# A vector sum issued four slots later, and a block pair's opening products issued ahead of a plain block

## The chip, the cores and the metric

The kernel runs on one core of a Trainium2 chip. The metric is the device time of one execution in microseconds. A core has a matrix engine (TensorE, PE in the profile; its weight loads are PEld), a vector engine (VectorE, DVE), a scalar engine (ScalarE, ACT), a general engine (GpSimd, POOL) and a queue engine for transfers (SyncE, SP). Each engine works through its own instructions in order, and semaphores tie the engines together.

## The reference

Two stages follow each other. The first is a linear attention over 8 batches, 8 heads, 576 positions and 64 features:

```python
q_p, k_p = phi(q), phi(k)          # relu, times cos and sin of the position
kv  = einsum('bhsf,bhsd->bhfd', k_p, v)
x   = einsum('bhsf,bhfd->bhsd', q_p, kv) / (q_p . sum_s(k_p) + 1e-6)
```

With the heads side by side, x is (8, 576, 512). The second stage mixes positions with a product of rank 32 and then applies two dense layers:

```python
u   = x + transpose(transpose(x) @ U @ V)
out = u + relu(u @ w_ch1) @ w_ch2          # 512 -> 2048 -> 512
```

## The kernel before

Matrix work is done in bf16 with float32 sums in PSUM, which has eight banks. The 576 positions of a batch are worked on as 512 (four chunks of 128) and a tail of 64; the tails of two batches go together.

**The order of the work** is written out by hand. The list `slots` holds steps for TensorE, and `put(n, ...)` hangs other steps behind slot n: VectorE sums, casts, attention units, transfers. At the end, a loop runs each slot, then what hangs behind it (in the order of the calls of `put`), then what `behind` has gathered. Within a slot, each engine receives its instructions in that order.

**The first dense layer** of batches 0 to 5 is made of plain blocks: `g1_main` (L569) makes one of 16 blocks of 128 hidden features with four matmuls of 512 columns (L579) and a relu on ScalarE (L588). The target banks turn over; at the place of the change they are g0 and g1.

For batch 6, `units` holds eight plain blocks (0, 8, 1, 9, 2, 10, 3 and 11) and, for the others, four *block pairs* p = 4 to 7 (block p with block p + 8). A block pair is one step of a scheme that multiplies 2 x 2 blocks with seven products instead of eight. `g1_cross` (L651) issues product i as two matmuls of 256 columns (L676). Products 1 and 2 go to the two halves X and Y of one bank, g0 or g1 by turns; products 6, 7 and 4 add to X later; 5 and 3 go to another bank. `g1_join` (L682) takes the results out: for "P1", ScalarE copies X to a buffer `kept` (L129); for "C11", VectorE adds that copy and Y (L611) into the hidden layer. `opened` issues products 1 and 2 and the joins P1 and C11; `sixth` issues product 6, again into X, and its copy. `third`, `fifth` and `closed` issue the rest.

The scheme needs sums of parts of its inputs, made on VectorE: `uT_sum` (L634, also L611 through `diff`) makes four of them from the transposed u, `w1_sum` those of the weights. `uT_s[b, 4]` is read by product 4 alone, which `closed` issues.

**The second dense layer** of the batch before, 5, runs between these steps: `half_part` (L862) issues eight matmuls of 256 columns (L891), and the same scheme gives it seven products for each half batch. `beside_g` puts one half part ahead of each unit. Its results are copied by ScalarE (L129) or added by VectorE (L847), and `hid_sum` (L833) makes sums of the hidden layer on VectorE.

**The attention of batch 7** runs in the same slots. `x_unit` (L415) issues eight matmuls of 65 columns (L422) into a tile of two banks that carries the name X too (another than the half X of a block pair) and exists once; VectorE takes the reciprocal (L412, L413) and multiplies (L432, into `x_tl` for the tail, into `x_bf` for the others), and after that the tile may be written again. Five of them follow each other, in every second slot; `A_unit` (L445) comes behind them.

With `at` the first slot of batch 6's first layer, a slot list of the stretch reads: `at + 4` a half part, `uT_sum(b6, 4)`, the tail's `x_unit`; `at + 6`, `at + 8`, `at + 10`, `at + 12` a half part and an `x_unit` each; `at + 13` the plain block 11 and the opening of block pair 4; `at + 14` a half part; `at + 15` product 6 of that pair and `A_unit`; `at + 19` the step `closed` of that pair.

Of the kernel before, what the change touches and what calls it, by code (L numbers as in the profile page):

```python
# [17 lines left out]
def kernel(  # L18
# [550 lines left out]
    def g1_main(b, j, half=False):  # L569
        if b not in hid:  # L570
            hid[b] = pool.tile([P, NJ, 512], BF16, tag="hid", bufs=2, name="hid")
        g_ps = g_open.pop((b, j), None)
        d0 = 0 if g_ps is None else 2
        if g_ps is None:
            g_ps = ps.tile([P, 512], FP32, tag="g", bufs=3, name="g_ps")
        if half:
            g_open[b, j] = g_ps
        for d in range(d0, 2 if half else 4):
            nc.tensor.matmul(  # L579
                out=g_ps.rearrange("p (c t) -> p c t", c=4),  # L580
                lhsT=w1_bf[:, d, j * P : j * P + P],
                rhs=uT[b][:, d, :, :],
                start=(d == 0),
                stop=(d == 3),
            )
        if half:
            return
        nc.scalar.activation(  # L588
            out=hid[b][:, j, :], in_=g_ps, func=AF.Relu, bias=0.0, scale=1.0
        )  # L590
# [19 lines left out]
    def diff(o, x, y, op=ALU.subtract):  # L610
        V_.tensor_tensor(out=o, in0=x, in1=y, op=op)  # L611
# [19 lines left out]
    def uT_quarter(b, d, n):  # L631
        return uT[b][:, 2 * d : 2 * d + 2, 2 * n : 2 * n + 2, :]

    def uT_sum(b, i):  # L634

        if not uT_s:
            t = pool.tile([P, 2, 4, 2, 2, P], BF16, tag="vst", bufs=1, name="uT_s")
            for n in range(4):
                for m in range(2):
                    uT_s[B - 2 + m, n + 1] = t[:, m, n]  # L640
        x, y = {
            1: lambda: (uT_quarter(b, 0, 1), uT_quarter(b, 0, 0)),
            2: lambda: (uT_quarter(b, 1, 1), uT_s[b, 1]),
            3: lambda: (uT_quarter(b, 1, 1), uT_quarter(b, 0, 1)),
            4: lambda: (uT_quarter(b, 1, 0), uT_s[b, 2]),
        }[i]()
        diff(uT_s[b, i], x, y)
# [3 lines left out]
    def g1_cross(b, p, i):  # L651

        if (b, p) not in cross:
            if b not in hid:
                hid[b] = pool.tile([P, NJ, 512], BF16, tag="hid", bufs=2, name="hid")
            of_x, of_z = CROSS[p % 2] if b == B - 1 else (("g0", "g1")[p % 2], "T")
            xy = psum.tile([P, 512], FP32, tag=of_x, bufs=1, name="c_ps")
            cross[b, p] = {"X": xy[:, 0:256], "Y": xy[:, 256:512], "of_z": of_z}  # L660
        w = cross[b, p]
        if i == 5:
            z = psum.tile([P, 512], FP32, tag=w["of_z"], bufs=1, name="c_ps")
            w["Z"] = z[:, 0:256]
        cs = slice(p * P, p * P + P)
        to, lhs, rhs, first = {
            1: lambda: ("X", W1[0], uT_quarter(b, 0, 0), True),
            2: lambda: ("Y", W1[1], uT_quarter(b, 1, 0), False),
            3: lambda: ("Z", w1_s[4], uT_quarter(b, 1, 1), False),
            4: lambda: ("X", W1[3], uT_s[b, 4], False),  # L670
            5: lambda: ("Z", w1_s[1], uT_s[b, 1], True),
            6: lambda: ("X", w1_s[2], uT_s[b, 2], False),
            7: lambda: ("X", w1_s[3], uT_s[b, 3], False),
        }[i]()
        for d in range(2):
            nc.tensor.matmul(  # L676
                out=w[to].rearrange("p (c t) -> p c t", c=2), lhsT=lhs[:, d, cs],
                rhs=rhs[:, d], start=(first and d == 0), stop=(d == 1),
                skip_group_check=not first,
            )  # L680

    def g1_join(b, p, i):  # L682

        w, lo, hi = cross[b, p], slice(0, 256), slice(256, 512)
        top, low = hid[b][:, p, :], hid[b][:, p + 8, :]

        def relu(o, x):
            nc.scalar.activation(out=o, in_=x, func=AF.Relu, bias=0.0, scale=1.0)

        if i == "C11":  # L690
            diff(top[:, lo], w["P1"], w["Y"], ALU.add)
        elif i == "C22":
            diff(low[:, hi], w["P5"], w["X"], ALU.add)
            relu(low[:, hi], low[:, hi])
        elif i == "C12":
            diff(top[:, hi], w["U2"], w["Z"], ALU.add)
            relu(low[:, lo], w["X"])
            V_.tensor_scalar(out=top, in0=top, scalar1=0.0, scalar2=None, op0=ALU.max)
        else:
            if (b, "kept") not in cross:  # L700
                cross[b, "kept"] = pool.tile(
                    [P, 2, 3, 256], FP32, tag="q_pT" if b == B - 1 else "q_p", bufs=1,
                    name="kept",
                )
            n = ("P1", "U2", "P5").index(i)
            w[i] = cross[b, "kept"][:, p % 2, n]
            cast(A_, w[i], w["Z" if i == "P5" else "X"])
# [630 lines left out]
    def put(at, thunk):  # L1338
        todo.setdefault(at, []).append(thunk)
# [11 lines left out]
    def g1(b, j):  # L1351
        return lambda: g1_main(b, j)
# [22 lines left out]
    for b in range(3, B - 2):  # L1375
        at = len(slots)
# [15 lines left out]
    b6, b7 = B - 2, B - 1  # L1392

    def opened(b, p):
        g1_cross(b, p, 1)
        g1_cross(b, p, 2)
        g1_join(b, p, "P1")
        g1_join(b, p, "C11")
# [24 lines left out]
    def crossed(*steps):  # L1423
        def go():
            for f, b, p in steps:
                f(b, p)

        return go
# [10 lines left out]
    at = len(slots)  # L1439
# [4 lines left out]
    ):  # L1444
        put(at + sl, lambda i=i, half=half: w1_sum(i, half))
    for i in range(4):
        put(at + 1 + i, lambda i=i: uT_sum(b6, i + 1))
    units = [g1(b6, j) for p in range(3) for j in (p, p + 8)] + [g1(b6, 3)]
    units.append(lambda: [g1_main(b6, 11), opened(b6, 4)])
    units.append(crossed((sixth, b6, 4)))  # L1450
    for p in range(5, 8):
        units.append(crossed((opened, b6, p), (fifth, b6, p - 1), (third, b6, p - 1)))
# [17 lines left out]
    at = len(slots)  # L1470
# [26 lines left out]
    at = len(slots)  # L1497
# [16 lines left out]
    at = len(slots)  # L1514
# [59 lines left out]
```

## Time and profile before

| | |
|---|---|
| median of three runs | 295.01 us (294.25 to 295.41) |
| the profiled execution's own time | 294.76 us |
| its span, first to last instruction | 293.0 us |
| granted TensorE clock | 1.000 |
| DMA | 56.18 MB, mean 192 GB/s |
| matmuls of L579 with 512 columns, into g_ps | 378, mean 379 ns |
| matmuls of L891 with 256 columns | some 273 ns each |

A row of the timeline gives the start and the duration in us, the engine, the line, the operation, output and inputs, and in brackets the idle time of the engine before it with what ended that. Ends of matmuls are modelled: a matmul's recorded duration reaches beyond the start of the next one, so the time that TensorE needs for a piece of work is read from one start to the next. The list of waits gives, for each pair of lines, the idle time in total, the number of times and the longest. The view of stretches gives, for a stretch, its length, the busy time of each engine with its count of instructions, the granted clock and the load of the DMA engines.

### The profile page before, as it was taken

The numbers are of one execution on the slowest core, as the hardware profiler recorded it, in microseconds if no ns is written. First come the engines' busy times: TensorE is split into PE (matmuls) and PEld (weight loads), VectorE is DVE, ScalarE is ACT, GpSimd is POOL, SyncE is SP. The second block draws the span as 40 slices with busy tenths as digits, with TensorE's granted clock in tenths as the row PEclk, the third lists the DMA queues.
The fourth block names the chain that finished last, engine by engine and source line by source line (L and its number), as shares of the span: only waits on it lengthen the run. The fifth ranks groups of instructions, "written<-read, shape, count | busy, mean of one in ns | idle before, by whom it ended". The sixth has DMA issues, their size and how long they took to land.

```text
span 293.0 us, 7309 instructions
## 1 busy us (share of the span) xinstructions
PE 284.9 (97%) x2910; PEld 194.5 (66%) x2944; DVE 206.6 (71%) x503; ACT 169.2 (58%) x353; POOL 56.6 (19%) x92
## 2 busy tenths in 40 slices
PE   8999999999999999999999999999999999999994
PEld 3775564447645446676767666766766888889883
DVE  5976766496876697657547793779957886765773
ACT  2955652176882767578736865497644555567210
POOL 5520400000020002301400501041101313303330
PEclk9999999999999999999999999999999999999999
DMA  6999999999988999999899939984902754336023
GB/s 210 304 254 251 260 163 223 223 332 251 316 178 135 312 231 246 232 313 268 128 231 273 272 72 292 214 284 87 219 2 38 120 116 98 64 93 142 4 103 116
DMA packets 95174, 56.18 MB, mean 192 GB/s; under 512 B 58692, under 2 KB 91844, under 8 KB 95140
## 3 DMA queue, kind: packets, MB, share of 16 engines
q1 hardware_dynamic: 84420, 43.94, 60.4%
q0 software_dynamic: 10528, 11.57, 19.5%
q8 instruction: 23, 0.38, 0.5%
q10 hardware_dynamic: 192, 0.20, 0.2%
q14 instruction: 11, 0.09, 0.1%
HBM read 36.86 MB, written 9.44 MB: 158 GB/s over the span
## 4 chain that ended last, share of the span: by engine, by line
PE 91%; ACT 3%; DMA 2%; DVE 2%; issue 1%; ACTq 0%; DVEq 0%
PE g_ps L579 29%; PE h_ps L891 26%; PE o_ps L759 10%; PE c_ps L676 7%; PE gt_ps L719 5%; PE kv_ps L347 3%; PE x_ps L422 3%; DMA qst<-in_q_dram 2%; PE a_ps L445 1%; PE h_ps L759 1%; PE g_ps L596 1%; PE va_ps L475 1%; PE t_ps L365 1%; ACT q_p L306 1%; ACT k_p L306 1%
## 5 line engine op out<-in xcount | busy, mean ns | idle before, releaser
L579 PE MATMUL g_ps<-uT,w_bf 128*128 128x512 bf16 x378 | 95.4, 379 | 1.2
L588 ACT ACTIVATE hid<-g_ps 128x512 bf16<-128x512 f32 x104 | 61.2, 598 | 58.8 <-PE g_ps L579 57.9
L579 PEld LDWEIGHTS <-w_bf 128*128 128x128 bf16 x402 | 37.5, 98 | 34.5 <-issue 0.2
L891 PEld LDWEIGHTS <-hid 128*128 128x128 bf16 x480 | 45.6, 98 | 9.5
L891 PE MATMUL h_ps<-w_bf,hid 128*128 128x256 bf16 x288 | 37.1, 273 | 0.0
L759 PE MATMUL o_ps<-w_bf,hid 128*128 128x512 bf16 x122 | 29.5, 379 | 0.4 <-issue 0.2
L891 PE MATMUL h_ps<-w_s,S 128*128 128x256 bf16 x208 | 26.5, 272 | 0.0
L131 POOL CAST v_ext<-vst 128x512 bf16<-128x512 f32 (+1 forms) x23 | 15.2, 689 | 58.1 <-DMA vst<-in_v_dram 30.3
L891 PE MATMUL h_ps<-w_s,hid 128*128 128x256 bf16 x192 | 24.9, 273 | 0.0
L847 DVE TENSOR_TENSOR o_sb<-o_sb,h_ps 128x256 f32<-128x256 f32 (+1 forms) x36 | 15.5, 432 | 12.2 <-PE h_ps L891 9.6
L891 PEld LDWEIGHTS <-S 128*128 128x128 bf16 x208 | 20.1, 98 | 4.4
L483 DVE TENSOR_TENSOR u_bf<-x_bf,va_ps 128x512 bf16<-128x512 bf16 x27 | 17.6, 680 | 6.5 <-PE va_ps L475 2.8
L950 POOL DMA_DIRECT2D out_dram<-o_sb x16 | 9.9, 617 | 63.3 <-DVE o_sb L847 50.4
L611 DVE TENSOR_TENSOR hid<-kept,c_ps 128x256 bf16<-128x256 f32 x36 | 14.2, 418 | 10.5 <-ACT kept L129 7.6
L847 DVE TENSOR_TENSOR o_sb<-u_bf,h_ps 128x256 f32<-128x256 bf16 x28 | 11.7, 417 | 13.6 <-PE h_ps L891 13.5
L759 PEld LDWEIGHTS <-hid 128*128 128x128 bf16 x128 | 11.5, 98 | 12.2
L949 POOL DMA_DIRECT2D o_sb<-u_bf x8 | 10.4, 1302 | 34.3 <-DVE rec L413 15.9
L719 PE MATMUL gt_ps<-uT_tl,w_bf 128*128 128x128 bf16 x256 | 16.2, 219 | 0.0
L432 DVE TENSOR_TENSOR x_bf<-x_ps,rec 128x512 bf16<-128x512 f32 x22 | 15.2, 691 | 0.8
L129 ACT ACTIVATE kept<-c_ps 128x256 f32<-128x256 f32 x36 | 12.5, 380 | 5.4 <-PE c_ps L676 5.0
L719 PEld LDWEIGHTS <-w_bf 128*128 128x128 bf16 x256 | 15.1, 98 | 0.7
L306 ACT ACTIVATE k_p<-kst,cosw 128x512 bf16<-128x512 f32 x20 | 14.2, 713 | 0.2 <-DMA kst<-in_k_dram 0.2
(189 smaller groups left out, 455.4 us busy)
## 6 DMA issues: line engine op xcount, KB each, us to landing
qst<-in_q_dram SPq DMA_DIRECT2D x14, 512.0 KB, 6.2
kst<-in_k_dram SPq DMA_DIRECT2D x14, 512.0 KB, 6.7
vst<-in_v_dram SPq DMA_DIRECT2D x12, 512.0 KB, 6.9
out_dram<-o_sb POOLq DMA_DIRECT2D x19, 256.0 KB, 3.9
out_dram<-o_sb SPq DMA_DIRECT2D x16, 256.0 KB, 2.6
w_bf<-in_moe_w_ch_dram POOLq DMA_DIRECT2D x7, 512.0 KB, 13.0
o_sb<-u_bf POOLq DMA_DIRECT2D x8, 256.0 KB, 3.7
qst<-in_q_dram SPq DMA_DIRECT2D x2, 640.0 KB, 14.2
```

The costliest lines, as they stand in the source:

```text
L131: eng.tensor_copy(out=o, in_=i)
L306: nc.scalar.activation(out=o, in_=i, func=AF.Relu, bias=0.0, scale=w)
L432: nc.vector.tensor_tensor(out=x_of(b, c, rows).rearrange("p (g i d) -> p g i d", g=2, d=D), in0=view[:, :, :, 0:D], in1=rec[rows].unsqueez ...
L483: nc.vector.tensor_tensor(out=u_bf[b][:, j, :, :], in0=x_bf[b][:, :, ns], in1=va[b][j].rearrange("p (c n) -> p c n", c=4), op=ALU.add,)
L579: nc.tensor.matmul(out=g_ps.rearrange("p (c t) -> p c t", c=4), lhsT=w1_bf[:, d, j * P : j * P + P], rhs=uT[b][:, d, :, :], start=(d == 0) ...
L588: nc.scalar.activation(out=hid[b][:, j, :], in_=g_ps, func=AF.Relu, bias=0.0, scale=1.0)
L611: V_.tensor_tensor(out=o, in0=x, in1=y, op=op)
L676: nc.tensor.matmul(out=w[to].rearrange("p (c t) -> p c t", c=2), lhsT=lhs[:, d, cs], rhs=rhs[:, d], start=(first and d == 0), stop=(d == 1 ...
L719: nc.tensor.matmul(out=g_ps[:, jj, :], lhsT=w1_bf[:, d, j * P : j * P + P], rhs=uT_tl[pr][:, d, :], start=(d == 0), stop=(d == 3),)
L759: nc.tensor.matmul(out=o[:, cols], lhsT=lhs[:, j, c * P : c * P + P], rhs=w2_bf[:, j, cols], start=(j == 0), stop=(j == NJ - 1),)
L847: eng.tensor_tensor(out=o, in0=x, in1=y, op=ALU.add)
L891: nc.tensor.matmul(out=acc, lhsT=lhs[:, j, :], rhs=rhs[:, j, :], start=(j == 0 and at is not None), stop=(j == 7), skip_group_check=at is ...
```

## The change

Two lines of the schedule differ. The sum `uT_sum(b6, 4)` hangs behind slot `at + 8` instead of `at + 4`. In slot `at + 13` the two steps change places: the four matmuls of `opened(b6, 4)` and its joins are issued first, then the four matmuls of plain block 11 and its relu.

```diff
     for i in range(4):
-        put(at + 1 + i, lambda i=i: uT_sum(b6, i + 1))
+        put(at + (1, 2, 3, 7)[i], lambda i=i: uT_sum(b6, i + 1))
     units = [g1(b6, j) for p in range(3) for j in (p, p + 8)] + [g1(b6, 3)]
-    units.append(lambda: [g1_main(b6, 11), opened(b6, 4)])
+    units.append(lambda: [opened(b6, 4), g1_main(b6, 11)])
     units.append(crossed((sixth, b6, 4)))
```

On TensorE, four matmuls of 256 columns with their weight loads now stand ahead of four of 512 columns. On ScalarE, the copy P1 stands ahead of the relu of block 11. On VectorE, the sum stands behind the first two attention products' reciprocals and multiplications and one sum of the hidden layer, ahead of the third's reciprocals. The instructions of GpSimd and SyncE keep their order.

## Prediction

> **What bounds the kernel now.** I read the page first, from the top: the busy time of the engines, then the chain of work that ended last.
>
> ```profile
> span 293.0 us, 7309 instructions
> ...
> PE 284.9 (97%) x2910; PEld 194.5 (66%) x2944; DVE 206.6 (71%) x503; ACT 169.2 (58%) x353; POOL 56.6 (19%) x92
> ...
> PE 91%; ACT 3%; DMA 2%; DVE 2%; issue 1%; ACTq 0%; DVEq 0%
> ```
>
> TensorE is busy for 97% of the span and makes up 91% of the chain. The change adds and removes no instruction, so all it can do is close holes in TensorE's stream or open new ones. So the next view is the list of waits, for TensorE alone, from 207 us to the end, the stretch that holds batch 6's first layer and everything behind it:
>
> ```profile
> PE c_ps L676 <- DVE hid L611: 0.4, 1, 0.4
> PE x_ps L422 <- DVE x_tl L432: 0.2, 1, 0.2
> ```
>
> Two waits, once each, and each stands beside one half of the diff. The third view is the timeline of all engines around them. The first hole (start in us, duration, engine, line; idle time before it in brackets):
>
> ```profile
> 214.55 0.42 PE L422 MATMUL x_ps<-kv,q_tlT 128*128 128x65 bf16 x8
> ...
> 214.81 0.42 DVE L847 TENSOR_TENSOR o_sb<-o_sb,h_ps 128x256 f32<-128x256 f32 x1 [2.27 <-ACT kv L129]
> ...
> 215.14 0.42 DVE L611 TENSOR_TENSOR uT_s<-uT,uT_s 128x512 bf16<-128x512 bf16 x1
> ...
> 215.59 0.17 DVE L412 TENSOR_SCALAR rec<-x_ps 64x8 f32<-64x8 f32 x1
> 215.67 1.04 PE L891 MATMUL h_ps<-w_s,S 128*128 128x256 bf16 x8
> ...
> 216.03 0.69 DVE L432 TENSOR_TENSOR x_tl<-x_ps,rec 64x512 bf16<-64x512 f32 x1
> ...
> 216.87 0.42 PE L422 MATMUL x_ps<-kv,q_pT 128*128 128x65 bf16 x8 [0.17 <-DVE x_tl L432]
> ...
> 217.92 0.69 DVE L432 TENSOR_TENSOR x_bf<-x_ps,rec 128x512 bf16<-128x512 f32 x1
> 217.99 1.04 PE L891 MATMUL h_ps<-w_s,S 128*128 128x256 bf16 x8
> ...
> 218.86 0.42 PE L422 MATMUL x_ps<-kv,q_pT 128*128 128x65 bf16 x8
> ...
> 219.32 0.17 DVE L412 TENSOR_SCALAR rec<-x_ps 128x8 f32<-128x8 f32 x1 [0.71 <-PE x_ps L422]
> ...
> 221.11 0.42 DVE L847 TENSOR_TENSOR o_sb<-o_sb,h_ps 128x256 f32<-128x256 f32 x1 [0.66 <-PE h_ps L891]
> ...
> 221.45 0.16 DVE L412 TENSOR_SCALAR rec<-x_ps 128x8 f32<-128x8 f32 x1
> ```
>
> Read TensorE's rows as a beat: one attention product (L422), four products of a plain block (L579), eight of a half part (L891). The view of stretches gives the length of two such beats, from one L422 to the next:
>
> ```profile
> 214.55:216.87 2.32, 2.10 (x21) 1.36 (x20) 1.93 (x6) 0.73 (x2) 0.00 (x0) 1.00 0.01 4
> 216.87:218.86 1.99, 1.99 (x20) 1.43 (x21) 1.64 (x4) 0.85 (x2) 0.00 (x0) 1.00 0.00 0
> 226.53:270.33 43.80, 43.80 (x457) 37.97 (x451) 31.95 (x81) 26.07 (x77) 11.57 (x11) 1.00 0.51 103
> ```
>
> The same work took 2.32 us in the first and 1.99 in the second: the hole is **0.33 us**, more than the 0.17 in the bracket, because modelled matmul ends run past the next start. In the second beat the eight products of L891 took 218.86 - 217.99 = 0.87, so without a wait the product at 216.87 would have begun at 215.67 + 0.87 = 216.54. It waited for the two-bank PSUM tile X, which VectorE emptied from 216.03 to 216.72; TensorE followed 0.15 later. And VectorE was late since the sum uT_s (215.14) stood between L847 and the reciprocals (215.59). The third row shows TensorE busy for all of the 43.80 us behind the second hole, at a granted clock of 1.00.
>
> The second hole:
>
> ```profile
> 221.11 1.02 PE L579 MATMUL g_ps<-uT,w_bf 128*128 128x512 bf16 x3
> ...
> 222.18 0.60 ACT L588 ACTIVATE hid<-g_ps 128x512 bf16<-128x512 f32 x1 [1.40 <-PE g_ps L579]
> ...
> 223.11 1.02 PE L579 MATMUL g_ps<-uT,w_bf 128*128 128x512 bf16 x4
> ...
> 223.85 0.69 DVE L432 TENSOR_TENSOR x_bf<-x_ps,rec 128x512 bf16<-128x512 f32 x1
> 223.97 0.60 PE L676 MATMUL c_ps<-uT,w_bf 128*128 128x256 bf16 x4
> 224.17 0.60 ACT L588 ACTIVATE hid<-g_ps 128x512 bf16<-128x512 f32 x1 [1.40 <-PE g_ps L579]
> ...
> 224.41 1.04 PE L891 MATMUL h_ps<-w_s,hid 128*128 128x256 bf16 x8
> 224.93 0.38 ACT L129 ACTIVATE kept<-c_ps 128x256 f32<-128x256 f32 x1 [0.17 <-ACT hid L588]
> ...
> 225.35 0.42 DVE L611 TENSOR_TENSOR hid<-kept,c_ps 128x256 bf16<-128x256 f32 x1 [0.80 <-ACT kept L129]
> ...
> 225.82 0.38 PE L676 MATMUL c_ps<-uT_s,w_s 128*128 128x256 bf16 x2 [0.38 <-DVE hid L611]
> ...
> 229.81 0.38 PE L676 MATMUL c_ps<-uT_s,w_bf 128*128 128x256 bf16 x2
> ```
>
> The block pair's first four products (223.97) fill both halves of bank g0. ScalarE copies one half (224.93), VectorE adds the other (225.35 to 225.77), and only then may TensorE write the bank again (225.82). What lies between is one half part of 0.87: it ended at 224.41 + 0.87 = 225.28, and the hole is 225.82 - 225.28 = **0.54 us**.
>
> **The change part by part.** *The sum moved, what is removed.* Elsewhere VectorE goes from L847 to the reciprocals in 221.45 - 221.11 = 0.34; here it took 215.59 - 214.81 = 0.78. So the sum cost 0.44, and without it the first reciprocal step starts at 215.15. Its data are there by then: from the start of an x_ps product to that step it takes 219.32 - 218.86 = 0.46 when VectorE is idle, here 214.55 + 0.46 = 215.01. X is then released 0.44 earlier, and the product could begin at 216.87 - 0.44 = 216.43. TensorE gets there at 216.54. The hole goes whole, **-0.33**, with 0.11 to spare; next in line is TensorE itself.
>
> A page's rule says less. The Trainium skill, "Perfetto Trace Analysis", section Optimizing Scalar/DVE Operations, holds that about 60 ns of a VectorE instruction's recorded latency overlap with the next one, so removing a record of 0.42 would free an estimated 0.36. By it the product could begin at 216.51 and the term would still be 0.33, with 0.03 to spare; the rows here say 0.44 for this place.
>
> *The sum moved, what is added.* It now stands ahead of the reciprocals of the third attention product. There VectorE sat idle for 0.71 (the bracket at 219.32), waiting for TensorE. The beat comes 0.33 earlier in the new kernel, and VectorE's work ahead of it 0.44 earlier, so the idle time is 0.71 + 0.11 = 0.82 and covers 0.44: cost 0. With no cover it would delay the reciprocals, and behind them the release of X, by up to 0.44. The sum's result is first read by the fourth product of the block pair, the row at 229.81; the sum is done near 218.7, 11 us before. The order of VectorE changes only in this; the queues of SP and POOL keep theirs, and no DMA is moved.
>
> *The block pair's first products in front.* Bank g0 gets its products at 223.11 instead of 223.97, and the plain block's four follow (0.86, from 223.11 to 223.97). All times here are still on the clock of before; the 0.33 shifts them together. ScalarE's copy could start as early as 223.11 + 0.60 (the products' modelled end), and I take as late a bound 224.93 - 223.97 = 0.96, the delay of before, in which it stood behind the relu at 224.17: at most 224.07. VectorE is occupied until 223.85 + 0.69 = 224.54 with the last attention product. The copy's start to the add took 225.35 - 224.93 = 0.42, so by ScalarE the add could begin at 224.49, by VectorE at 224.54: VectorE decides. The add's start to TensorE's took 225.82 - 225.35 = 0.47, so the bank is free at 225.01. TensorE, after four c_ps products (224.41 - 223.97 = 0.44), the plain block (0.86) and the half part (0.87), comes there at 223.11 + 2.17 = 225.28. So the second hole goes too, **-0.54**, with 0.27 to spare.
>
> A rule speaks against that cover. The Trainium skill, "TensorE: Matmul & The Clock Gate", section Back-to-back issue gap, gives a sustained 131 ns for a 512-column matmul. The plain block would be an estimated 0.52 instead of 0.86, the cover would end at 224.94, and 0.07 of the hole would stay (term 0.47). The trace disagrees: four such matmuls take 0.86, or 0.215 each.
>
> What is late next: the plain block's relu, which stood at 224.17, is now behind the copy, at about 223.55 + 1.06 = 224.61 (1.06 from block to relu, 224.17 - 223.11). Nothing near reads it. The opening products need g0 empty: the relu of the block before ends at 222.18 + 0.60 = 222.78, and 0.15 of signalling (as at the first hole) makes 222.93, so 0.18 are to spare. That wait had the plain block in front of it as cover; now it has none.
>
> **Sum:** -0.33 - 0.54 = -0.87 us. Behind it TensorE stands without a hole to 270.33, and its own chain sets the end, so it carries through. The profiled execution took 294.76 us (span 293.0 and 1.76 around it); 294.76 - 0.87 = 293.89. It lies 0.25 under the median of 295.01 of the three runs, so on the median I forecast 295.01 - 0.87 = **294.14 us**, 0.3% faster. About 0.5% (1.5 us) is what a measurement of this kernel can tell from no change, so that counts as the same.
>
> **The rivals.** *Only one hole closes.* The margins are 0.11 and 0.27, both on VectorE, and signalling could eat the first. Then it is 295.01 - 0.54 = 294.47, or 294.68 with the first alone. For it: the first margin is under one semaphore's 0.15. Against: both terms come from rows of the same shape close by.
>
> *The gain is given back, or the change does not do what it says.* If something with a time of its own, such as a transpose or a store, sat just behind TensorE, 0.87 us of lead would turn into a new wait: 295.0 us. Against: not one wait is recorded in the 43.80 us behind, and the transposes of batch 7 start from VectorE's results, which come earlier as well.
>
> *Slower, by bank g0.* The place is 223.11, where the opening products now stand first and need the relu that ended at 222.78. From 0.18 us of delay of that relu on, TensorE stops, one for one, and with it the plain block and the half part behind, in order. It eats the 0.87 once the relu is 0.18 + 0.87 = 1.05 late: two more ScalarE pieces of 0.60 ahead of it would do, 1.20 late, a stop of 1.02 and 295.01 + 0.15 = 295.16 us. Against: that relu began at 222.18, 0.05 behind the modelled end of its block (221.11 + 1.02 = 222.13), so nothing of ScalarE stood in front of it.
>
> **How the numbers follow.** Both holes close: 0.73. One: 0.15. Given back or without effect: 0.08. Slower by g0: 0.04. The predicted time is the first case's. The unknowns there are small (0.11 + 0.27 of margin), but the three runs reach 0.76 below and 0.40 above their median, so the range goes from 294.14 - 0.74 = 293.4 up to 295.1, which takes in all cases but the last part of the slower one. Faster by over 0.5% means under 293.53, 0.61 below the forecast: about one in ten, from the spread in the first case, 0.09. Slower by over 0.5% needs 296.5, beyond each price above: 0.03. The rest, 0.88, is within 0.5%.
>
> **What would show it.** In the changed kernel's list of TensorE's waits, both rows should be gone; the two beats of L422 should both be 1.99; from the half part behind the plain block to the next c_ps product it should be 0.87 instead of 1.41; and VectorE's idle time ahead of the third attention product's reciprocals should shrink by about 0.33, to some 0.4. The stretch behind, up to 270.33, should keep its 43.80 us. The forecast is wrong if a wait on ScalarE stands ahead of the first c_ps products, if L422's wait for L432 comes back one or two products later, or if the stretch behind grows by what was won.

## The result and the profile after

The changed kernel took 293.56 us in the median of 7 runs (293.05 to 294.23), the kernel before 295.19 (294.21 to 296.46); the ratio is 0.9949, with a 95% interval of 0.9927 to 0.9971. A second comparison on one chip, with 12 and 35 runs, gave 293.89 against 294.82 and a ratio of 0.9969 (0.9949 to 0.9989). The forecast, 294.14 on 295.01, is a ratio of 0.9971: the second comparison gives the 0.3% that was forecast, the first 0.5%, with an interval that just reaches it.

The page of the changed kernel, profiled in an execution of 294.23 us, with the rows that were shown of before:

```profile
span 292.4 us, 7343 instructions
...
PE 287.0 (98%) x2944; PEld 194.7 (67%) x2944; DVE 206.7 (71%) x503; ACT 169.3 (58%) x353; POOL 56.4 (19%) x92
...
PE 98%; DVE 1%; issue 0%; DVEq 0%
```

The 34 instructions more on TensorE are none of the kernel's: some matmul records were missing from the trace of before (both pages have 2944 weight loads). The chain's 98% in place of 91% has nothing to do with the change either: over the first 15 us the chain of before is followed back through a transfer and ScalarE's work, that of the changed kernel through TensorE's. The list of TensorE's waits, taken over the whole span, has one row left, from the program's first microseconds; both rows of the stretch from 207 us on are gone:

```profile
PE w_ps L234 <- DVE zero L141: 1.2, 1, 1.2
```

The timeline of the changed kernel at the place of the first hole:

```profile
214.88 0.42 PE L422 MATMUL x_ps<-kv,q_tlT 128*128 128x65 bf16 x8
...
215.14 0.42 DVE L847 TENSOR_TENSOR o_sb<-o_sb,h_ps 128x256 f32<-128x256 f32 x1 [2.27 <-ACT kv L129]
...
215.59 0.17 DVE L412 TENSOR_SCALAR rec<-x_ps 64x8 f32<-64x8 f32 x1
...
216.00 1.04 PE L891 MATMUL h_ps<-w_s,S 128*128 128x256 bf16 x8
216.03 0.69 DVE L432 TENSOR_TENSOR x_tl<-x_ps,rec 64x512 bf16<-64x512 f32 x1
...
216.87 0.42 PE L422 MATMUL x_ps<-kv,q_pT 128*128 128x65 bf16 x8
...
217.92 0.69 DVE L432 TENSOR_TENSOR x_bf<-x_ps,rec 128x512 bf16<-128x512 f32 x1
...
218.52 0.42 DVE L611 TENSOR_TENSOR uT_s<-uT,uT_s 128x512 bf16<-128x512 bf16 x1
...
218.87 0.42 PE L422 MATMUL x_ps<-kv,q_pT 128*128 128x65 bf16 x8
...
219.32 0.17 DVE L412 TENSOR_SCALAR rec<-x_ps 128x8 f32<-128x8 f32 x1 [0.39 <-PE x_ps L422]
```

At 216.87 no idle time stands in brackets: 216.00 + 0.87 is when TensorE gets there. So the tile was free by then, but only just. TensorE's weight loads for the two products show it:

```profile
216.84 0.33 PEld L422 LDWEIGHTS <-q_pT 128*128 128x128 bf16 x8
...
218.76 0.40 PEld L422 LDWEIGHTS <-q_pT 128*128 128x128 bf16 x8
```

The second starts 0.11 ahead of its product (218.87), the first only 0.03 ahead (216.87). The sum has moved to 218.52, and the idle time ahead of the third product's reciprocals has shrunk from 0.71 to 0.39. At the place of the second hole:

```profile
222.18 0.60 ACT L588 ACTIVATE hid<-g_ps 128x512 bf16<-128x512 f32 x1 [1.40 <-PE g_ps L579]
...
222.85 0.42 PE L422 MATMUL x_ps<-kv,q_pT 128*128 128x65 bf16 x8
...
223.11 0.60 PE L676 MATMUL c_ps<-uT,w_bf 128*128 128x256 bf16 x4
...
223.55 1.03 PE L579 MATMUL g_ps<-uT,w_bf 128*128 128x512 bf16 x4
...
223.80 0.38 ACT L129 ACTIVATE kept<-c_ps 128x256 f32<-128x256 f32 x1 [1.02 <-PE c_ps L676]
...
223.86 0.69 DVE L432 TENSOR_TENSOR x_bf<-x_ps,rec 128x512 bf16<-128x512 f32 x1
...
224.41 1.04 PE L891 MATMUL h_ps<-w_s,hid 128*128 128x256 bf16 x8
224.47 0.41 DVE L611 TENSOR_TENSOR hid<-kept,c_ps 128x256 bf16<-128x256 f32 x1
224.61 0.60 ACT L588 ACTIVATE hid<-g_ps 128x512 bf16<-128x512 f32 x1 [0.43 <-PE g_ps L579]
...
225.28 0.38 PE L676 MATMUL c_ps<-uT_s,w_s 128*128 128x256 bf16 x2
```

The opening products (223.11) come first, the plain block (223.55) and the half part (224.41) run while ScalarE copies and VectorE adds, and product 6 starts at 225.28, with no wait: 224.41 + 0.87. The view of stretches, for the two beats and for the work behind:

```profile
214.88:216.87 1.99, 1.99 (x22) 1.37 (x20) 1.60 (x5) 0.60 (x1) 0.00 (x0) 1.00 0.02 4
216.87:218.87 2.00, 2.00 (x23) 1.44 (x22) 1.90 (x5) 0.98 (x2) 0.00 (x0) 1.00 0.00 0
225.99:269.80 43.81, 43.81 (x459) 37.95 (x451) 31.60 (x81) 26.14 (x77) 11.58 (x11) 1.00 0.56 106
```

Both beats now take 2 us, and the stretch behind has kept its length, 43.81 us after 43.80.

**A yardstick.** Up to batch 7's tail attention product (L422 from q_tlT, 214.55 before and 214.88 after) the instructions of both kernels are the same. So I measure from the start of that row to the start of the last eight L891 products of the execution: 287.80 - 214.55 = 73.25 us before, 287.26 - 214.88 = **72.38** after, that is 0.87 less. The changed kernel reached that row 0.33 later than the one before, which hides a third of the gain in the spans (293.0 and 292.4) and has nothing to do with the change.

### The profile page after: what moved, and what is told of

Read it like the earlier page. It is cut to its first block, busy times and chain, and to the rows that moved or that the text cites. A ratio compares the mean times of both kernels' runs of the same rounds, so it can differ in the third digit from the quotient of the medians.

```text
span 292.4 us, 7343 instructions
## 1 busy us (share of the span) xinstructions
PE 287.0 (98%) x2944; PEld 194.7 (67%) x2944; DVE 206.7 (71%) x503; ACT 169.3 (58%) x353; POOL 56.4 (19%) x92
## 4 chain that ended last, share of the span: by engine, by line
PE 98%; DVE 1%; issue 0%; DVEq 0%
PE g_ps L579 30%; PE h_ps L891 27%; PE o_ps L759 10%; PE c_ps L676 7%; PE gt_ps L719 5%; PE w_ps L234 3%; PE kv_ps L347 3%; PE x_ps L422 3%; PE a_ps L445 1%; PE h_ps L759 1%; PE g_ps L596 1%; PE va_ps L475 1%; PE t_ps L377 1%; PE t_ps L365 1%; PE z_ps L1236 1%; PE kv_ps L1132 0%
## 5 line engine op out<-in xcount | busy, mean ns | idle before, releaser
L579 PE MATMUL g_ps<-uT,w_bf 128*128 128x512 bf16 x402 | 97.3, 379 | 0.0
L891 PEld LDWEIGHTS <-hid 128*128 128x128 bf16 x480 | 45.6, 98 | 9.7
L891 PE MATMUL h_ps<-w_bf,hid 128*128 128x256 bf16 x288 | 37.1, 273 | 0.0
L759 PE MATMUL o_ps<-w_bf,hid 128*128 128x512 bf16 x128 | 30.1, 379 | 0.0
L891 PE MATMUL h_ps<-w_s,S 128*128 128x256 bf16 x208 | 26.5, 272 | 0.0
L891 PE MATMUL h_ps<-w_s,hid 128*128 128x256 bf16 x192 | 24.9, 273 | 0.0
L847 DVE TENSOR_TENSOR o_sb<-o_sb,h_ps 128x256 f32<-128x256 f32 (+1 forms) x36 | 15.5, 432 | 12.2 <-PE h_ps L891 9.6
L891 PEld LDWEIGHTS <-S 128*128 128x128 bf16 x208 | 20.1, 98 | 4.4
L847 DVE TENSOR_TENSOR o_sb<-u_bf,h_ps 128x256 f32<-128x256 bf16 x28 | 11.7, 417 | 13.5 <-PE h_ps L891 13.4
```

The source lines that it names most:

```text
L579: nc.tensor.matmul(out=g_ps.rearrange("p (c t) -> p c t", c=4), lhsT=w1_bf[:, d, j * P : j * P + P], rhs=uT[b][:, d, :, :], start=(d == 0) ...
L759: nc.tensor.matmul(out=o[:, cols], lhsT=lhs[:, j, c * P : c * P + P], rhs=w2_bf[:, j, cols], start=(j == 0), stop=(j == NJ - 1),)
L847: eng.tensor_tensor(out=o, in0=x, in1=y, op=ALU.add)
L891: nc.tensor.matmul(out=acc, lhsT=lhs[:, j, :], rhs=rhs[:, j, :], start=(j == 0 and at is not None), stop=(j == 7), skip_group_check=at is ...
```

## The experiments

Theory A: the two holes are all that the change moves, and each edit closes one. The rivals (B) are named with each run. "The stretch" is the yardstick, 73.25 before and 72.38 after.

**The changed kernel again.** No edit.

> The changed kernel once more, beside the kernel before. The stretch from batch 7's tail attention product (L422, q_tlT) to the start of the last eight L891 products was 73.25 us before and 72.38 in the changed kernel's first profile. Theory A, the two holes are all of it: the stretch is 72.38 again to 0.05, whatever the whole execution does, and the median of whole executions lies 0.9 us (0.3%) below the one before, within the scatter of 0.4 to 0.8 us that the medians have. Theory B, the change is worth what the medians first showed (295.19 to 293.56, 1.6 us), with some 0.8 us from outside the two holes: the median is again 1.4 to 1.9 us below, and the part ahead of that tail product is shorter in the changed kernel by some 0.7 us.

The stretch was 286.59 - 214.21 = 72.38, and the medians 293.89 and 294.82, 0.93 apart. That is A; the 1.63 between the first medians was 0.87 and scatter. Where the scatter comes from can be seen in the profiles. The instructions ahead of the tail product are the same in all of them but for their place in time, and over all the executions told here that row began anywhere from 214.10 to 215.84 (the kernels with a relu made three times, and twice in the old order).

**The sum alone.**

```diff
-        put(at + 1 + i, lambda i=i: uT_sum(b6, i + 1))
+        put(at + (1, 2, 3, 7)[i], lambda i=i: uT_sum(b6, i + 1))
```

> Only the sum is moved; the plain block stays ahead of the opening products. Theory A: the first hole closes (0.33) and the second stays (0.54 on the c_ps products of product 6), so the stretch from the tail product to the last L891 group is 73.25 - 0.33 = 72.92. Theory B, the two edits work together: the sum alone gives less than 0.2, or closes the second hole too (72.38).

The stretch was 288.08 - 215.16 = 72.92, and TensorE's list from 200 us on keeps one row:

```profile
PE c_ps L676 <- DVE hid L611: 0.4, 1, 0.4
```

**The order alone.**

```diff
-    units.append(lambda: [g1_main(b6, 11), opened(b6, 4)])
+    units.append(lambda: [opened(b6, 4), g1_main(b6, 11)])
```

> Only the opening products are put first; the sum stays in its old slot. Theory A: the second hole closes (0.54), the first stays (0.33, with L422's wait for L432 in the list), so the stretch is 73.25 - 0.54 = 72.71. Theory B: the swap alone leaves part of its hole, since VectorE is late by what the sum cost it; the stretch is then 72.8 to 73.2.

The stretch was 287.24 - 214.53 = 72.71, and the list, from 207 us on, keeps the other row:

```profile
PE x_ps L422 <- DVE x_tl L432: 0.2, 1, 0.2
```

So each edit closes its own hole, 0.33 and 0.54, whether the other is there or not, and they add up to 0.87. The times of whole executions, 294.58 (ratio 0.9987, 0.9969 to 1.0006) and 294.35 (0.9986, 0.9966 to 1.0006), can't tell either from no change; the stretch can.

**The sum two slots later in place of four.**

```diff
-        put(at + (1, 2, 3, 7)[i], lambda i=i: uT_sum(b6, i + 1))
+        put(at + (1, 2, 3, 5)[i], lambda i=i: uT_sum(b6, i + 1))
```

> The changed kernel, but with the sum two slots later than before in place of four: ahead of the second attention product's reciprocals. Theory A, the idle time at the fourth slot is what makes the move free: here VectorE has none, the reciprocals start 0.44 later, the tile of the attention products is released at about 219.20 on the changed kernel's clock where TensorE comes at 218.87, so the hole is back one beat later with 0.33 and the stretch is 72.38 + 0.33 = 72.71. Theory B, it only matters that the sum leaves the tail product's place: no hole, 72.38.

The stretch was 287.29 - 214.76 = 72.53, 0.15 more than 72.38: the hole is back, but smaller than A had it. The timeline of this kernel:

```profile
216.63 0.69 DVE L833 TENSOR_TENSOR hid<-hid,S 128x1024 bf16<-128x1024 bf16 x1
...
217.24 0.42 DVE L611 TENSOR_TENSOR uT_s<-uT,uT_s 128x512 bf16<-128x512 bf16 x1
...
217.69 0.17 DVE L412 TENSOR_SCALAR rec<-x_ps 128x8 f32<-128x8 f32 x1
217.88 1.04 PE L891 MATMUL h_ps<-w_s,S 128*128 128x256 bf16 x8
...
218.13 0.69 DVE L432 TENSOR_TENSOR x_bf<-x_ps,rec 128x512 bf16<-128x512 f32 x1
...
218.88 0.43 PE L422 MATMUL x_ps<-kv,q_pT 128*128 128x65 bf16 x8
```

TensorE would have come to the product at 217.88 + 0.87 = 218.75 and started at 218.88, a hole of 0.13 (the rest of the 0.15 lies in the next beats). From L833 to the reciprocals it is 217.69 - 216.63 = 1.06 where the changed kernel has 0.73, so here the sum cost 0.33, not the 0.44 of the expectation. And TensorE began 0.06 behind the end of VectorE's multiplication (218.13 + 0.69 = 218.82), not the 0.15 of the first hole. The two make up 0.11 + 0.09 = 0.20, by which A's hole of 0.33 was too large. The whole execution, 294.07 against 294.82 (ratio 0.9973, 0.9955 to 0.9991), can't tell 0.15. The place counts, as A says; the price of the sum and the time from the release to TensorE's start were set too high.

The five runs that follow are of one execution each, and single times of whole executions say nothing about some tenths of a microsecond; only their stretch and rows are read.

**The relu that empties bank g0 made twice**, in the new order. Its second write gives the same values.

```diff
-        nc.scalar.activation(
+        [nc.scalar.activation(
             out=hid[b][:, j, :], in_=g_ps, func=AF.Relu, bias=0.0, scale=1.0
-        )
+        ) for _ in range(2 if (b, j) == (B - 2, 3) else 1)]
```

> The changed kernel with the relu of plain block 3 of batch 6, which empties bank g0, made twice in a row (the second writes the same values again), so that the bank is free some 0.55 us later. Theory A, the opening products now stand first and have lost the plain block as cover: they wait for that relu from a delay of 0.18 on, so TensorE gets a hole of 0.55 - 0.18 = 0.37 ahead of them, put down to ScalarE L588, and the stretch from the tail product to the last L891 group is 72.38 + 0.37 = 72.75. Theory B, the opening products' place costs nothing since the wait ends early anyway or the bank is another one: no hole, 72.38.

The stretch was 287.35 - 214.63 = 72.72, and the wait is there:

```profile
221.93 1.23 ACT L588 ACTIVATE hid<-g_ps 128x512 bf16<-128x512 f32 x2 [1.40 <-PE g_ps L579]
...
222.61 0.42 PE L422 MATMUL x_ps<-kv,q_pT 128*128 128x65 bf16 x8
...
223.21 0.60 PE L676 MATMUL c_ps<-uT,w_bf 128*128 128x256 bf16 x4 [0.18 <-ACT hid L588]
```

Without it the opening products would have begun 0.26 after the attention product (223.11 - 222.85 in the changed kernel), at 222.87; the hole is 0.34. The second relu took 1.23 - 0.60 = 0.63, so 0.63 - 0.34 = 0.29 of delay were free. A wait of a new kind, on ScalarE, has taken the place of the plain block's cover, as the slower rival had it.

**The same relu three times** (3 in the place of 2).

> The changed kernel with that relu made three times. Theory A, beyond 0.18 us of delay TensorE stops one for one: the hole is 0.37 + 0.55 = 0.92, the stretch 73.30, so that the gain of 0.87 is just eaten. Theory B: 72.38, or a hole that does not grow with the third relu.

The stretch was 287.46 - 214.10 = 73.36, 0.98 over 72.38 and a little over the kernel before, at a delay of 1.86 - 0.60 = 1.26:

```profile
221.40 1.86 ACT L588 ACTIVATE hid<-g_ps 128x512 bf16<-128x512 f32 x3 [1.40 <-PE g_ps L579]
...
222.07 0.42 PE L422 MATMUL x_ps<-kv,q_pT 128*128 128x65 bf16 x8
...
223.31 0.60 PE L676 MATMUL c_ps<-uT,w_bf 128*128 128x256 bf16 x4 [0.82 <-ACT hid L588]
```

1.26 - 0.98 = 0.28 free again, and 0.64 more of hole for 0.63 more of delay: one for one.

**The relu twice in the old order**, the plain block ahead of the opening products, the sum moved.

> The same doubled relu with the plain block ahead of the opening products as before, and the sum at its new place. Theory A: the plain block's 0.86 covers the delay, no wait for ScalarE L588 appears ahead of the opening products, only the second hole of 0.54 stands, and the stretch is 72.92, as with the sum alone. Theory B, the delay costs the same in either order: 73.3.

The stretch was 288.48 - 215.84 = 72.64. No wait for ScalarE ahead of the opening products, as A has it; but the second hole had shrunk from 0.54 to 0.27 (product 6 at 226.51, TensorE there at 225.37 + 0.87), which neither theory foresaw. The list of waits has no row for it: a hole of this size is nearly covered by the modelled ends. One thing differs besides the delay: the second relu waits for the first, and with that the copy P1 no longer carries a wait for ScalarE's own earlier work. The next run asks whether that is the cause.

**An earlier relu twice in the old order**, that of plain block 10, where ScalarE has idle time to spare.

```diff
-        ) for _ in range(2 if (b, j) == (B - 2, 3) else 1)]
+        ) for _ in range(2 if (b, j) == (B - 2, 10) else 1)]
```

> Where the doubled relu stood in the old order, the second hole shrank from 0.54 to 0.27 us, unforeseen. Here the doubled relu is that of plain block 10, two blocks earlier, in the old order with the sum moved; ScalarE idles there, so the doubling itself delays nothing. It carries a wait of ScalarE for its own earlier instructions, after which the copy P1 needs none and carries its wait for TensorE itself, in place of a separate semaphore instruction ahead of it. Theory A, the copy lost 0.27 by coming late behind the relu of block 11 through that separate instruction: the copy starts 0.49 after that relu's start instead of 0.77, the hole is 0.27, and the stretch from the tail product to the last L891 group is 72.92 - 0.27 = 72.65. Theory B, the smaller hole came from the later relu of block 3 next to it: the copy starts 0.77 after the relu, the hole is 0.54, the stretch 72.92.

The stretch was 287.53 - 214.88 = 72.65, as A has it. By chance the rows of this place fall on the same times as before, so they can be laid beside those of the prediction:

```profile
224.17 0.60 ACT L588 ACTIVATE hid<-g_ps 128x512 bf16<-128x512 f32 x1 [1.40 <-PE g_ps L579]
...
224.41 1.04 PE L891 MATMUL h_ps<-w_s,hid 128*128 128x256 bf16 x8
224.66 0.38 ACT L129 ACTIVATE kept<-c_ps 128x256 f32<-128x256 f32 x1
225.07 0.42 DVE L611 TENSOR_TENSOR hid<-kept,c_ps 128x256 bf16<-128x256 f32 x1 [0.53 <-ACT kept L129]
...
225.55 0.38 PE L676 MATMUL c_ps<-uT_s,w_s 128*128 128x256 bf16 x2
```

The relu of block 11 begins at 224.17 in both. The copy follows at 224.66 here and at 224.93 before, and product 6 at 225.55 and 225.82. ScalarE's queue shows what differs. Rows of its semaphore instructions for the line of the copy, around it; first the kernel before, then this one (count, then shortest, median and longest in ns):

```profile
L129 ACTq EVENT_SEMAPHORE  x2: 17/198/379, 224.2 to 224.2; - x2
```

```profile
L129 ACTq EVENT_SEMAPHORE  x1: 38/38/38, 224.2 to 224.2; - x1
```

In the program of before, the copy has four waits: one for a DMA queue stands in a first semaphore instruction, one for another queue and the one for TensorE in a second, and the copy itself waits only for an older ScalarE instruction, long done (the bracket of its row in the prediction names the relu of block 11, but the wait is for one far ahead of it). The second semaphore instruction blocks ScalarE's queue for 0.379, until the opening products are done; the copy comes too late to run into the end of the relu, and starts 0.16 behind it. In this kernel one semaphore instruction holds both waits for the queues, and the copy carries the wait for TensorE itself and overlaps the relu's end by 0.11 (224.17 + 0.60 - 224.66). So half of the second hole was the wait itself, and half that semaphore instruction. That the doubled relu takes the wait off the copy, and that this closes 0.27, is shown; that lateness behind the relu is how the time is lost is the reading that fits the rows.

**The sum five times at its new place.** The other four write the same values.

```diff
-        put(at + (1, 2, 3, 7)[i], lambda i=i: uT_sum(b6, i + 1))
+        put(at + (1, 2, 3, 7)[i], lambda i=i: uT_sum(b6, i + 1)); i == 3 and [put(at + 8, lambda: uT_sum(b6, 4)) for _ in range(4)]
```

> The changed kernel with the moved sum made five times at its new place (the other four write the same values again). VectorE idles there for 0.39 after one sum, and the tile's release lies 0.26 ahead of TensorE's next product. Theory A, the place has room for one sum and about 0.65 us more: four more sums of 0.33 to 0.44 take 1.3 to 1.8, so the hole ahead of the fourth attention product is 0.7 to 1.1 and the stretch 73.1 to 73.5. Theory B, VectorE has room for any such work in this stretch: no hole, 72.38.

The stretch was 288.58 - 214.96 = 73.62, 1.24 more, a little over A's range:

```profile
218.60 2.25 DVE L611 TENSOR_TENSOR uT_s<-uT,uT_s 128x512 bf16<-128x512 bf16 x5
...
220.07 1.04 PE L891 MATMUL h_ps<-w_s,hid 128*128 128x256 bf16 x8
...
220.77 0.16 DVE L412 TENSOR_SCALAR rec<-x_ps 128x8 f32<-128x8 f32 x1
...
221.21 0.69 DVE L432 TENSOR_TENSOR x_bf<-x_ps,rec 128x512 bf16<-128x512 f32 x1
...
222.04 0.42 PE L422 MATMUL x_ps<-kv,q_pT 128*128 128x65 bf16 x8 [0.94 <-DVE x_bf L432]
```

The hole is 222.04 - (220.07 + 0.87) = 1.10. Each repeated sum took (2.25 - 0.42) / 4 = 0.46, since each waits for the one before it, more than the 0.33 to 0.44 of the expectation. Of the added 2.25 - 0.42 = 1.83, 1.83 - 1.10 = 0.73 cost nothing, near the 0.65 of the expectation; beyond that VectorE sets TensorE's beat.

The other 0.14 appear near 238 us, at a hole that every one of these kernels has. In the changed kernel it reads:

```profile
236.18 0.75 DVE L611 TENSOR_TENSOR hid<-kept,c_ps 128x256 bf16<-128x256 f32 x2
...
236.60 0.39 PE L676 MATMUL c_ps<-uT,w_s 128*128 128x256 bf16 x2
...
236.98 0.38 PE L676 MATMUL c_ps<-uT_s,w_bf 128*128 128x256 bf16 x2
```

Products 3 and 4 of a later block pair start 0.38 apart, where two such matmuls take 0.22 (the next ones start at 237.20). Product 4 follows the end of VectorE's two joins (236.18 + 0.75 = 236.93) by 0.05. No list of waits shows this hole of 0.16, since the modelled ends cover it. With the five sums VectorE comes to the joins later, and the two products are 238.30 - 237.78 = 0.52 apart.

## Why the prediction was right

**Two holes, and their sizes.** Both terms came out to the hundredth, 0.33 and 0.54, together and one by one. What made this possible was to measure a hole from start to start: the bracketed idle times, 0.17 and 0.38, would have given 0.55 in place of 0.87. For the same reason the two vanished rows of the list of waits would not have been enough as proof; the stretch is.

**The sum removed.** The term was right, its working was not, and that the hole closed whole was luck. The prediction had the sum cost 0.44 and the tile free 0.11 before TensorE. In the changed kernel the reciprocals come 215.59 - 215.14 = 0.45 behind L847, not the 0.34 taken from another place, so the sum had cost 0.78 - 0.45 = 0.33. The tile was emptied at 216.72, and the 0.15 of signalling of the old hole would put the product at 216.87, where TensorE came: no margin was left, as the weight load shows that starts only 0.03 ahead of it. The step that failed is the start-to-start time taken from another place. The input was no readier there: the attention product starts 0.26 ahead of L847 at both (220.86 and 221.12, 214.88 and 215.14 in the changed kernel). Why the tail's reciprocals follow L847 0.11 later than a full chunk's stays open. The rule of the Trainium skill ("Perfetto Trace Analysis", Optimizing Scalar/DVE Operations), an estimated 0.36, was nearer than the row, and the run with the sum two slots later measured 0.33 again.

**The sum added.** Idle time of 0.39 was left where 0.38 was forecast; the price of the sum, 0.11 too high, and the lead of VectorE's work, 0.11 too large, cancel in that sum. The runs with the sum two slots later and five times show that cost 0 belongs to this place and not to VectorE: two slots earlier the same sum costs TensorE 0.13, and at the new place four more cost 1.10.

**The opening products in front.** VectorE's last attention product set the add, as forecast: 224.47 against 224.54. The bank came free at 224.47 + 0.47 = 224.94, 0.34 before TensorE in place of 0.27. The copy came 0.69 after the products, not the 0.96 taken as a bound from before. The difference is the semaphore instruction: in the run with the earlier relu twice the copy also comes 224.66 - 223.97 = 0.69 after them, with the relu ahead of it. So half of the old hole came from something that the prediction had not seen; its term held all the same, since the new order covers the whole wait. The relu of block 11 fell on 224.61, the forecast time. The Trainium skill's rule ("TensorE: Matmul & The Clock Gate", Back-to-back issue gap), 131 ns for a 512-column matmul, fails here: the plain block takes 224.41 - 223.55 = 0.86.

**The rivals.** One hole alone: the two runs with one edit show those times, but only because the other edit was taken out. Given back: the stretch behind kept 43.8 us. That it holds no hole was too strong, since the start-to-start times show one of 0.16 to 0.17 near 237 us in both kernels (237.13 to 237.52 before); it kept its size, so it took nothing. The slower one, by bank g0, was a real mechanism with the right law, one for one; the delay that costs nothing is 0.28 to 0.29, not 0.18, since the opening products follow the relu by 0.05 (221.93 + 1.23 to 223.21), not by the 0.15 assumed from the first hole, where a semaphore instruction stands in between (last section). The relu wasn't late, so it didn't come to it.

**The time.** 294.14 was forecast from a median of three; the medians measured, 293.56 and 293.89, lie 0.6 and 0.25 lower, with the interval of the first ratio (0.9927 to 0.9971) reaching just to the forecast. By that first ratio the gain is a little over 0.5%, which the prediction had given about one in ten; the 0.87 of the stretch says that the rest was scatter. The range from the spread of the runs was the right caution: the arrival at the first changed instruction alone varies by 1.7 us.

## What to carry to other kernels

When the engine that sets the time is busy almost throughout, read its holes from start to start against an undisturbed beat nearby; the bracketed idle time is too small. A step that only has to be done some time should stand in the idle time of its engine, and a step whose result passes through other engines ahead of work that needs nobody; check what else that order uncovers, here the release of a bank. And for changes far below the scatter of whole executions, take the stretch between two instructions that both kernels share: it came out the same to 0.01 us in two executions of one kernel, where whole runs differ by 1 us and more.

## What the runs showed of the hardware

A wait for TensorE that stood in a semaphore instruction ahead of a ScalarE copy cost 0.27 us when ScalarE was busy with another piece at the time (copy 0.76 after the relu's start, with the wait in the copy itself 0.49); when ScalarE had nothing running, in the changed kernel, the copy followed the products' modelled end by 0.09 (223.11 + 0.60 to 223.80) with that same semaphore instruction.

TensorE followed the release of a PSUM bank by 0.05 to 0.06 us at ScalarE's relu (both runs with repeated relus), at VectorE's joins (225.77 to 225.82 before, 236.93 to 236.98 after) and at VectorE's multiplication in the run with the sum two slots later (218.82 to 218.88). It followed by 0.14 to 0.15 at the first hole (216.72 to 216.87) and in the run with five sums (221.90 to 222.04). At these two a semaphore instruction of 51 ns stands ahead of the product's first weight load, and at none of the others; for the first hole:

```profile
L422 PEldq EVENT_SEMAPHORE  x1: 51/51/51, 216.8 to 216.8; - x1
```

No run takes that instruction away with all else the same. That it makes the whole difference fits the rows and is not shown.
